# Another order of steps in a chunked attention followed by a multiplicative FFN: S and P of pairs 0 to 3, 6 and 7, turns of x, and some loads

## The chip, the core and the metric

The kernel runs on one core of a Trainium2 chip. The metric is the device time of one execution in microseconds (us). The core's engines run side by side, each through its own list of instructions in order: PE (matrix products, which it writes to PSUM), DVE and ACT (elementwise work), POOL and SP (here they mostly issue DMAs). They wait for each other by semaphores.

## The reference, cut to what matters

```
q, k, v: (8, 8, 576, 64)              # batch, heads, sequence, head size
in chunks of 64 tokens (9 per sequence), per head:
    attn = exp(scores) / (sum + 1e-09),  scores = q @ k.T / 8  (less the row's maximum)
    out  = attn @ v
x = out of all heads side by side      # (4608, 512)
a, b = x @ w1, x @ w2                  # w1, w2: (512, 1024)
result = ((a * b) @ w3) @ w_out        # w3: (1024, 1024), w_out: (1024, 512)
```

## The kernel before, in words

The 4608 tokens are cut into 18 **pairs** of 256 tokens (four chunks). The kernel is one list of steps, `ORDER` (lines 9 to 40), that line 447 goes through; each step issues its instructions at once, and on every engine they run in the order of the list. Nothing else schedules the work: a step that stands earlier in the list stands earlier on each engine that it uses. A letter names the kind of step, the first number is the pair p (or a group of two pairs g = p // 2), the second a part.

| step | engine | what it does (line) |
|---|---|---|
| R0, R1, K0, K1 | SP, ACT | load q and k of pair 0 without a cast, and cast them (135, 141) |
| q, k, v | POOL | loads of a pair, cast to bf16 on the way, in one to three DMAs each (149, 165) |
| i0 to i3, o, h0, h1 | POOL | a quarter of w1 and of w2, w_out, a half of w3 (428, 180, 433) |
| x | POOL | a tiny copy that makes POOL wait until the pair's xn is there (161) |
| T p.0, T p.1 | DVE | turn q and k in blocks of 32 x 32 (195) |
| G g | SP | eight moves that bring the turned blocks together, for pairs 8 and up (205) |
| S p | PE | scores; 64 products of 32 rows (pairs 0 to 7) or 32 of 64 rows (214) |
| E p | ACT | exp (231) |
| P p | PE | exp times v, and the row's sum; 64 or 32 products, in two halves (238) |
| N p.u | DVE | a reciprocal and a product, giving half a pair of x (258) |
| X p.u | DVE | turn half a pair of x (293) |
| H g | SP | eight moves of turned x, for pairs 8 and up (310) |
| A, B p.f | PE | a block of x @ w1, of x @ w2: 8 products of 256 columns for pairs 0 to 3, 4 of 512 for two pairs at a time from pair 4 (326) |
| C p.f | ACT | copy A's result out of PSUM (349) |
| M p.f | DVE | a * b into `ab` (353) |
| V, W, Z | DVE, PE, ACT | turn w3, compute w3 @ w_out once, store it as `w3o` (405 to 420) |
| O p, Y p, Q p | PE, ACT, SP | 16 products of `ab` and `w3o`, the copy out of PSUM, the store (377 to 402) |
| D | PE | filler: products of zeros into a PSUM tile that the next step overwrites (318); D0.1.0.4.512 are 4 of 512 columns |

Five things set who waits for whom:

- **PSUM.** All PSUM tiles come from one pool of four slots (lines 88 and 101). A step that opens a tile waits until the last reader of a slot has run. S is freed by E, each half of P by its N, A and B (one tile) by M, O by Y, W by Z.
- **C and B share a tile.** C reads the half that A wrote. Where C stands ahead of B in the list, PE waits for the copy before B.
- **Buffers in SBUF.** Copies of A have three buffers (line 350), outputs `o_sb` two (395), so Y of one pair waits until the store two before it has landed. q and k have five, v six.
- **POOL's loads.** Each load waits until the load eight before it has landed.
- **SP's queue.** G, H and Q go out in order; a store behind moves leaves after them.

The whole of O16 and O17 stands at the end; O17 goes out in three parts, so that the last store is small. `second_path` (line 453) runs only where a sum was out of range, which it is not here.

Of the kernel before, what the change touches and what calls it, by code (L numbers as in the profile page):

```python
# [7 lines left out]

ORDER = """
R0 R1 v0 q1 k1 i0 v1 i1 i2 q2 k2 v2 i3 q3 k3 v3 q4 k4 v4 o h0 h1 D0.0.0.16.64 K0 T0.0 K1 T0.1 q5 k5  # L10
v5 S0 T1.0 E0 P0 D0.1.0.4.512 T1.1 q6 k6 v6 N0.0 S1 D1.0.0.5.512 X0.0 N0.1 X0.1 A0.0 E1 B0.0 C0.0 P1
M0.0 A0.1 N1.0 X1.0 B0.1 C0.1 N1.1 A0.2 X1.1 B0.2 C0.2 M0.1 A1.0 T2.0 B1.0 C1.0 M0.2 A1.1 T2.1 q7 k7
v7 B1.1 C1.1 M1.0 S2 M1.1 A0.3 E2 T3.0 B0.3 C0.3 P2 M0.3 A1.2 N2.0 X2.0 B1.2 C1.2 N2.1 A1.3 X2.1
B1.3 C1.3 M1.2 A2.0 T3.1 q8 k8 v8 B2.0 C2.0 M1.3 S3 T4.0 A2.1 E3 M2.0 B2.1 T4.1 q9 k9 C2.1 P3 v9
M2.1 A2.2 N3.0 B2.2 C2.2 X3.0 A2.3 N3.1 B2.3 X3.1 C2.3 M2.2 S4 M2.3 A3.0 E4 B3.0 C3.0 A3.1 M3.0 B3.1
C3.1 V0 A3.2 M3.1 B3.2 C3.2 V1 A3.3 M3.2 B3.3 C3.3 V2 W0 M3.3 V3 W1 Z0 V4 V5 W2 Z1 V6 V7 T5.0 Z2 W3
T5.1 q10 k10 T6.0 T6.1 P4 v10 q11 k11 Z3 S5 N4.0 O0 E5 X4.0 N4.1 X4.1 T7.0 O1 T7.1 Y0 Q0 T8.0 P5 v11
q12 k12 Y1 S6 T8.1 O2 Q1 E6 N5.0 X5.0 N5.1 X5.1 O3 T9.0 T9.1 Y2 G4.0 P6 v12 q13 k13 A4.0 N6.0 B4.0
G4.1 Y3 X6.0 N6.1 C4.0 A4.1 X6.1 B4.1 C4.1 M4.0 Q2 S7 Q3 M4.1 A4.2 E7 T10.0 B4.2 C4.2 T10.1 P7 v13
q14 k14 A4.3 M4.2 B4.3 N7.0 C4.3 A4.4 X7.0 M4.3 B4.4 C4.4 N7.1 A4.5 M4.4 B4.5 C4.5 X7.1 S8 M4.5 S9  # L20
E8 A4.6 T11.0 B4.6 E9 T11.1 P8 v14 q15 k15 C4.6 A4.7 M4.6 G5.0 B4.7 C4.7 N8.0 A6.0 M4.7 B6.0 N8.1
C6.0 G5.1 A6.1 X8.0 B6.1 M6.0 C6.1 X8.1 P9 v15 A6.2 M6.1 N9.0 B6.2 C6.2 N9.1 A6.3 M6.2 B6.3 C6.3
X9.0 A6.4 M6.3 B6.4 C6.4 X9.1 A6.5 T12.0 H4.0 B6.5 C6.5 M6.4 A6.6 M6.5 B6.6 T12.1 H4.1 C6.6 S10 S11
M6.6 E10 A6.7 T13.0 B6.7 E11 P10 T13.1 C6.7 O4 M6.7 G6.0 N10.0 N10.1 X10.0 G6.1 P11 Y4 X10.1 O5
N11.0 N11.1 x11 q16 k16 v16 Q4 X11.0 X11.1 T14.0 A8.0 H5.0 Y5 B8.0 T14.1 C8.0 A8.1 M8.0 B8.1 H5.1
C8.1 T15.0 A8.2 B8.2 M8.1 C8.2 T15.1 Q5 A8.3 B8.3 C8.3 M8.2 G7.0 S12 M8.3 S13 E12 A8.4 T16.0 B8.4
E13 G7.1 P12 T16.1 C8.4 A8.5 B8.5 M8.4 C8.5 N12.0 A8.6 M8.5 B8.6 C8.6 N12.1 x12 q17 k17 v17 A8.7
M8.6 B8.7 C8.7 X12.0 P13 M8.7 A10.0 X12.1 B10.0 C10.0 N13.0 A10.1 M10.0 B10.1 N13.1 C10.1 A10.2
X13.0 B10.2 M10.1 C10.2 X13.1 S14 S15 M10.2 E14 A10.3 H6.0 T17.0 B10.3 E15 P14 T17.1 C10.3 A10.4
H6.1 M10.3 B10.4 C10.4 N14.0 A10.5 M10.4 B10.5 G8.0 C10.5 N14.1 A10.6 M10.5 B10.6 C10.6 X14.0 P15  # L30
G8.1 X14.1 A10.7 M10.6 B10.7 N15.0 C10.7 O6 N15.1 M10.7 X15.0 X15.1 H7.0 S16 Y6 S17 O7 E16 E17 H7.1
P16 Y7 O8 Q6 N16.0 Q7 N16.1 X16.0 X16.1 P17 Y8 A12.0 N17.0 Q8 B12.0 N17.1 C12.0 A12.1 X17.0 B12.1
M12.0 C12.1 X17.1 A12.2 M12.1 H8.0 B12.2 C12.2 A12.3 M12.2 B12.3 C12.3 H8.1 A12.4 M12.3 B12.4 C12.4
A12.5 M12.4 B12.5 C12.5 A12.6 M12.5 B12.6 C12.6 A12.7 M12.6 B12.7 C12.7 O9 M12.7 O10 Y9 Q9 A14.0 Y10
B14.0 C14.0 Q10 A14.1 M14.0 B14.1 C14.1 A14.2 M14.1 B14.2 C14.2 A14.3 M14.2 B14.3 C14.3 A14.4 M14.3
B14.4 C14.4 A14.5 M14.4 B14.5 C14.5 A14.6 M14.5 B14.6 C14.6 A14.7 M14.6 B14.7 C14.7 O11 M14.7 O12
Y11 Q11 A16.0 Y12 B16.0 C16.0 Q12 A16.1 M16.0 B16.1 C16.1 A16.2 M16.1 B16.2 C16.2 A16.3 M16.2 B16.3
C16.3 A16.4 M16.3 B16.4 C16.4 A16.5 M16.4 B16.5 C16.5 A16.6 M16.5 B16.6 C16.6 A16.7 M16.6 B16.7
C16.7 O13 M16.7 O14 Y13 Q13 O15 Y14 Q14 O16 Y15 Q15 Y16 Q16 O17
"""  # L40


# [525 lines left out]
```

## Time and profile before

| | |
|---|---|
| median of 3 runs | 244.46 us (244.37 to 244.63) |
| profiled execution | 244.48 us, of which the span of the profile is 242.9 |
| PE busy | 226.7 us, 2753 products |
| DVE, ACT, POOL busy | 154.3, 85.2, 83.7 us |
| granted PE clock | 1.0 over the span |
| 71 copies C, 586 ns each | 41.6 us of ACT |
| 71 products M, 674 ns each | 47.8 us of DVE |
| 36 turns T, 1291 ns each | 45.1 us of DVE |
| chain that ended last | PE 72%, DMA 16%, DVE 4%, SP's queue 3% |

How to read the views: a timeline line gives start, length, engine, source line, operation, tiles written and read, and the number of instructions merged; in brackets stands the idle time of the engine just before it and what ended it. "Issue" is idle time for which the profile shows no releaser. All products have one source line, that of a helper, so the tile names tell the steps apart: `z_ps` are the fillers and the tiles that they opened, `s_ps` S, `pv` P, `ab_ps` A and B, `o_ps` O, `qkT` T, `xt` and `xm` X. Source lines are those of this kernel; the changed list is one line shorter.

### The profile page before, as it was taken

Reading aid. Unit: us, or ns where it says so; the run is one execution under the profiler, and the core shown is the slowest. Engines: PE = TensorE matmul, PEld = TensorE weight load, DVE = VectorE, ACT = ScalarE, POOL = GpSimd, SP = SyncE. Lnnn points to the kernel's source line nnn. Section 1 sums busy time; section 2 is a strip of 40 time slices with the busy share of each in tenths; the row PEclk is TensorE's granted clock in tenths of the full one; section 3 lists DMA queues with packets and bytes.
Section 4 is the critical chain, followed back from the end, with each engine's and each line's share of the span. In section 5 each row is a group of like instructions: output and inputs, shape, how many; then the busy total and the mean of one; then the engine's idle time right before and its main releaser. Section 6 shows DMA issues by size and latency. Waiting matters only on the chain.

```text
span 242.9 us, 6385 instructions
## 1 busy us (share of the span) xinstructions
PE 226.7 (93%) x2753; PEld 120.2 (49%) x2753; DVE 154.3 (64%) x235; ACT 85.2 (35%) x116; POOL 83.7 (34%) x114
## 2 busy tenths in 40 slices
...
GB/s 173 179 185 181 185 169 200 196 193 171 167 173 218 222 228 259 179 224 196 205 236 223 221 139 91 163 88 209 142 0 89 87 0 0 173 3 1 86 173 173
DMA packets 93597, 37.65 MB, mean 155 GB/s; under 512 B 75008, under 2 KB 86528, under 8 KB 93568
## 3 DMA queue, kind: packets, MB, share of 16 engines
...
q8 instruction: 21, 0.34, 0.6%
...
## 4 chain that ended last, share of the span: by engine, by line
PE 72%; DMA 16%; DVE 4%; SPq 3%; POOL 2%; issue 1%; ACT 0%; DVEq 0%; POOLq 0%
PE ab_ps L95 39%; PE o_ps L95 23%; PE w_ps L95 6%; DMA w<-in_moe_w_dram 4%; DMA qkm<-qkT 3%; SPq L193 3%; DMA qk<-in_q_dram 3%; DMA qk<-in_k_dram 3%; DMA xt<-xm 3%; PE pv L95 2%; PE s_ps L95 2%; DVE qkT L201 2%; POOL vbuf L98 1%; POOL w L98 1%; DVE xt L297 1%
## 5 line engine op out<-in xcount | busy, mean ns | idle before, releaser
L95 PE MATMUL ab_ps<-xt,w 128*128 128x512 bf16 (+1 forms) x688 | 127.4, 342 | 0.7 <-DVE xt L297 0.6
L95 PEld LDWEIGHTS <-w 128*128 128x128 bf16 x704 | 67.1, 98 | 56.1 <-issue 1.8
L366 DVE TENSOR_TENSOR ab<-a_sb,ab_ps 128x512 bf16<-128x512 f32 x71 | 47.8, 674 | 43.4 <-ACT a_sb L351 43.1
L351 ACT COPY a_sb<-ab_ps 128x512 f32<-128x512 f32 x71 | 41.6, 586 | 81.3 <-PE ab_ps L95 81.0
L95 PE MATMUL o_ps<-w3o,ab 128*128 128x512 bf16 (+1 forms) x296 | 63.9, 373 | 0.0
L201 DVE STREAM_TRANSPOSE qkT<-qk 128x1024 bf16<-128x1024 bf16 x36 | 45.1, 1291 | 7.2 <-ACT qk L144 5.5
L95 PEld LDWEIGHTS <-ab 128*128 128x128 bf16 x296 | 28.5, 98 | 32.2
L98 POOL DMA_DIRECT2D vbuf<-in_v_dram x40 | 33.9, 855 | 20.4 <-DMA qk<-in_q_dram 5.2
L396 ACT COPY o_sb<-o_ps 128x1024 f32<-128x1024 f32 x17 | 17.2, 1012 | 45.3 <-PE o_ps L95 41.3
L264 DVE TENSOR_TENSOR xn<-pv,rcs 128x512 bf16<-128x512 f32 x36 | 24.9, 692 | 1.4
...
L234 ACT ACTIVATE e<-s_ps 128x1024 bf16<-128x1024 f32 x16 | 15.9, 1026 | 1.7 <-PE s_ps L95 1.3
L95 PE MATMUL w_ps<-wo,w3T 128*128 128x512 bf16 x64 | 14.0, 379 | 0.0
L305 DVE STREAM_TRANSPOSE xm<-xn 128x512 bf16<-128x512 bf16 x20 | 13.5, 696 | 0.2
L261 DVE RECIPROCAL rcs<-pv 128x8 f32<-128x8 f32 x36 | 6.9, 193 | 10.4 <-PE pv L95 10.4
L98 POOL DMA_DIRECT2D w<-in_moe_w_dram x16 | 11.1, 695 | 5.3 <-DMA wo<-in_moe_w_out_dram 2.9
...
L95 PE MATMUL pv<-vbuf,e 64*32 64x65 bf16 (+1 forms) x832 | 10.2, 197 | 1.8 <-ACT e L234 1.1
L297 DVE STREAM_TRANSPOSE xt<-xn 128x512 bf16<-128x512 bf16 x16 | 11.4, 711 | 0.5
L389 DVE COPY o_sb<-o_ps 128x256 f32<-128x256 f32 x1 | 0.4, 425 | 16.0 <-PE o_ps L95 16.0
L95 PEld LDWEIGHTS <-qkT 32*64 32x64 bf16 x512 | 5.5, 117 | 10.1 <-DVE qkT L201 7.9
...
## 6 DMA issues: line engine op xcount, KB each, us to landing
...
```

The source lines that it names most:

```text
L95: return inorder(nc.tensor.matmul(*a, **kw))
L98: return inorder(nc.gpsimd.dma_start(dst, src))
L193: inorder(nc.sync.dma_start(dst, src))
L201: inorder(nc.vector.transpose(qkT_t[g][:, :, p % 2, s, heads(h)].rearrange("p e h (y t) -> p h t e y", t=2), qk_t[p][:, s, heads(h)].rearr ...
L234: inorder(nc.scalar.activation(e_t[p][:, :, heads(hh)], s_t[p][:].rearrange("p u (h q) -> p u h q", q=CH)[:, :, heads(hh)], Exp, scale=sca ...
L261: inorder(nc.vector.reciprocal(rc, pv[:, :, :, D:W]))
L264: inorder(nc.vector.tensor_mul(xn_t[p][:, u], pv[:, :, :, 0:D], rc.to_broadcast([P, 2, 4, D])))
L297: inorder(nc.vector.transpose(new_xt(g)[:].rearrange("p (o t) -> p o t", o=KO)[:, :, t0:t0 + UT] .rearrange("p o (m y) -> p m o y", y=BL), ...
L305: inorder(nc.vector.transpose(xm_t[g][:, u, :, m].rearrange("p o (c y) -> p c o y", y=BL), xn_t[p][:].rearrange("p u r m d -> p (u r) m d" ...
L351: inorder(nc.scalar.copy(a_t[p, j][:], ps_t[p, j][:, 0, :]))
L366: inorder(nc.vector.tensor_mul(o, view(a_t.pop((p, j))[:]), view(ps_t.pop((p, j))[:, 1, :])))
L396: inorder(nc.scalar.copy(o_sb[:], ps_t.pop(p)[:]))
```

## The change

Only the list changes. The 606 steps stay the same but for the three fillers: D0.0.0.16.64 becomes D0.0.0.24.64 and stands ahead of h0, D0.1.0.4.512 becomes D0.1.0.6.512, D1.0.0.5.512 becomes D1.0.0.1.512 and stands ahead of P0. In the order:

- S and P of pairs 0 to 3, 6 and 7 change places with blocks A and B: S1 stands behind A0.0, P1 behind A0.1, S2 behind A0.3, P2 behind A1.2, S7 behind A4.2, P7 behind A4.3; likewise P8 behind A4.6, P12 behind A8.5, P14 behind A10.4, P17 behind A12.0.
- Turns X, and N, stand ahead of some products M: both N of pair 2 ahead of both X, X1.1 ahead of M0.0, X15.0 and X15.1 ahead of M10.7, X16 and X17.1 ahead of M12.0.
- Blocks change places (A1.1 ahead of A1.0, A8.3 ahead of A8.1, O10 inside A12's blocks, O14 inside A16's), and six copies C stand ahead of their B (1.0, 1.2, 1.3, 3.3, 6.0, 8.3).
- Turns T change places (T6.1 ahead of T5.0, T13.1 ahead of T13.0 and T12.1, T17.0 ahead of M10.2, X5.0 behind T9), and V6 ahead of V4. E4 stands behind Z2, E13 ahead of E12, Y14 ahead of Y13.
- Loads change places from k6 on (k6 ahead of v5 and q6, v11 ahead of k11, k12 ahead of q12, v12 behind q13, q16, k16 and v16 ahead of x11, k17 behind v17); Q3 stands ahead of Q2 on SP.

The diff, cut to the stretches where these stand:

```
--- before
+++ after
-R0 R1 v0 q1 k1 i0 v1 i1 i2 q2 k2 v2 i3 q3 k3 v3 q4 k4 v4 o h0 h1 D0.0.0.16.64 K0 T0.0 K1 T0.1 q5 k5
-v5 S0 T1.0 E0 P0 D0.1.0.4.512 T1.1 q6 k6 v6 N0.0 S1 D1.0.0.5.512 X0.0 N0.1 X0.1 A0.0 E1 B0.0 C0.0 P1
-M0.0 A0.1 N1.0 X1.0 B0.1 C0.1 N1.1 A0.2 X1.1 B0.2 C0.2 M0.1 A1.0 T2.0 B1.0 C1.0 M0.2 A1.1 T2.1 q7 k7
-v7 B1.1 C1.1 M1.0 S2 M1.1 A0.3 E2 T3.0 B0.3 C0.3 P2 M0.3 A1.2 N2.0 X2.0 B1.2 C1.2 N2.1 A1.3 X2.1
-B1.3 C1.3 M1.2 A2.0 T3.1 q8 k8 v8 B2.0 C2.0 M1.3 S3 T4.0 A2.1 E3 M2.0 B2.1 T4.1 q9 k9 C2.1 P3 v9
+R0 R1 v0 q1 k1 i0 v1 i1 i2 q2 k2 v2 i3 q3 k3 v3 q4 k4 v4 o D0.0.0.24.64 h0 h1 K0 T0.0 K1 T0.1 q5 S0 E0
+T1.0 T1.1 k5 D1.0.0.1.512 k6 v5 P0 q6 N0.0 D0.1.0.6.512 X0.0 N0.1 X0.1 A0.0 S1 E1 B0.0 C0.0 A0.1 v6 P1
+N1.0 X1.0 N1.1 X1.1 M0.0 B0.1 T2.0 A0.2 C0.1 B0.2 T2.1 C0.2 M0.2 q7 A1.1 A1.0 C1.0 B1.1 v7 B1.0 C1.1
+M1.0 M1.1 M0.1 A0.3 S2 T3.0 B0.3 E2 k7 C0.3 M0.3 A1.2 P2 C1.2 A1.3 N2.0 v8 N2.1 X2.0 X2.1 B1.2 C1.3 T3.1
+B1.3 A2.0 q8 k8 B2.0 S3 C2.0 M1.2 A2.1 M1.3 T4.0 E3 M2.0 B2.1 P3 T4.1 q9 v9 A2.2 N3.0 C2.1 B2.2 A2.3
...
-T5.1 q10 k10 T6.0 T6.1 P4 v10 q11 k11 Z3 S5 N4.0 O0 E5 X4.0 N4.1 X4.1 T7.0 O1 T7.1 Y0 Q0 T8.0 P5 v11
-q12 k12 Y1 S6 T8.1 O2 Q1 E6 N5.0 X5.0 N5.1 X5.1 O3 T9.0 T9.1 Y2 G4.0 P6 v12 q13 k13 A4.0 N6.0 B4.0
-G4.1 Y3 X6.0 N6.1 C4.0 A4.1 X6.1 B4.1 C4.1 M4.0 Q2 S7 Q3 M4.1 A4.2 E7 T10.0 B4.2 C4.2 T10.1 P7 v13
-q14 k14 A4.3 M4.2 B4.3 N7.0 C4.3 A4.4 X7.0 M4.3 B4.4 C4.4 N7.1 A4.5 M4.4 B4.5 C4.5 X7.1 S8 M4.5 S9
-E8 A4.6 T11.0 B4.6 E9 T11.1 P8 v14 q15 k15 C4.6 A4.7 M4.6 G5.0 B4.7 C4.7 N8.0 A6.0 M4.7 B6.0 N8.1
+N4.0 S5 Z3 T6.0 E5 T7.1 q11 X4.0 O0 N4.1 X4.1 T8.0 Y0 Q0 T7.0 O1 P5 Y1 v11 S6 O2 N5.0 k11 T8.1 k12 N5.1
+E6 X5.1 Q1 O3 q12 T9.1 T9.0 G4.0 k13 P6 X5.0 A4.0 Y2 q13 B4.0 G4.1 N6.0 Y3 N6.1 X6.0 C4.0 A4.1 B4.1 X6.1
+v12 A4.2 C4.1 M4.0 Q3 M4.1 Q2 S7 E7 B4.2 C4.2 A4.3 P7 T10.0 T10.1 q14 B4.3 v13 M4.2 N7.0 A4.5 X7.0 C4.3
+A4.4 M4.3 B4.4 C4.4 B4.5 C4.5 N7.1 k14 X7.1 M4.4 S8 S9 M4.5 E8 q15 A4.6 P8 T11.0 B4.6 T11.1 k15 E9 C4.6
+M4.6 A4.7 N8.0 B4.7 C4.7 A6.0 A6.1 v14 M4.7 N8.1 G5.0 X8.0 C6.0 G5.1 B6.0 B6.1 M6.0 C6.1 M6.1 P9 v15
...
-X13.0 B10.2 M10.1 C10.2 X13.1 S14 S15 M10.2 E14 A10.3 H6.0 T17.0 B10.3 E15 P14 T17.1 C10.3 A10.4
...
-G8.1 X14.1 A10.7 M10.6 B10.7 N15.0 C10.7 O6 N15.1 M10.7 X15.0 X15.1 H7.0 S16 Y6 S17 O7 E16 E17 H7.1
-P16 Y7 O8 Q6 N16.0 Q7 N16.1 X16.0 X16.1 P17 Y8 A12.0 N17.0 Q8 B12.0 N17.1 C12.0 A12.1 X17.0 B12.1
+B10.1 A10.2 k17 C10.1 X13.0 M10.1 B10.2 C10.2 S14 S15 A10.3 E14 X13.1 H6.0 T17.0 M10.2 B10.3 E15 A10.4
+T17.1 H6.1 C10.3 P14 G8.0 B10.4 M10.3 N14.0 C10.4 A10.5 M10.4 B10.5 N14.1 C10.5 A10.6 G8.1 B10.6 M10.5
+X14.1 C10.6 X14.0 P15 A10.7 B10.7 O6 M10.6 C10.7 N15.0 N15.1 X15.0 X15.1 H7.0 S16 S17 E16 O7 P16 M10.7
+Y6 E17 Y7 H7.1 O8 A12.0 Q6 P17 A12.1 N16.0 Q7 Y8 N16.1 N17.0 B12.0 N17.1 X16.0 A12.2 X16.1 Q8 C12.0
...
```

More of the change, by code (lines that the diff above doesn't have):

```diff
@@ L15 @@
-M2.1 A2.2 N3.0 B2.2 C2.2 X3.0 A2.3 N3.1 B2.3 X3.1 C2.3 M2.2 S4 M2.3 A3.0 E4 B3.0 C3.0 A3.1 M3.0 B3.1
-C3.1 V0 A3.2 M3.1 B3.2 C3.2 V1 A3.3 M3.2 B3.3 C3.3 V2 W0 M3.3 V3 W1 Z0 V4 V5 W2 Z1 V6 V7 T5.0 Z2 W3
-T5.1 q10 k10 T6.0 T6.1 P4 v10 q11 k11 Z3 S5 N4.0 O0 E5 X4.0 N4.1 X4.1 T7.0 O1 T7.1 Y0 Q0 T8.0 P5 v11
-q12 k12 Y1 S6 T8.1 O2 Q1 E6 N5.0 X5.0 N5.1 X5.1 O3 T9.0 T9.1 Y2 G4.0 P6 v12 q13 k13 A4.0 N6.0 B4.0
-G4.1 Y3 X6.0 N6.1 C4.0 A4.1 X6.1 B4.1 C4.1 M4.0 Q2 S7 Q3 M4.1 A4.2 E7 T10.0 B4.2 C4.2 T10.1 P7 v13
@@ L20 @@
-q14 k14 A4.3 M4.2 B4.3 N7.0 C4.3 A4.4 X7.0 M4.3 B4.4 C4.4 N7.1 A4.5 M4.4 B4.5 C4.5 X7.1 S8 M4.5 S9
-E8 A4.6 T11.0 B4.6 E9 T11.1 P8 v14 q15 k15 C4.6 A4.7 M4.6 G5.0 B4.7 C4.7 N8.0 A6.0 M4.7 B6.0 N8.1
[L22 to L25, printed above, removed]
@@ L26 @@
-C8.1 T15.0 A8.2 B8.2 M8.1 C8.2 T15.1 Q5 A8.3 B8.3 C8.3 M8.2 G7.0 S12 M8.3 S13 E12 A8.4 T16.0 B8.4
-E13 G7.1 P12 T16.1 C8.4 A8.5 B8.5 M8.4 C8.5 N12.0 A8.6 M8.5 B8.6 C8.6 N12.1 x12 q17 k17 v17 A8.7
-M8.6 B8.7 C8.7 X12.0 P13 M8.7 A10.0 X12.1 B10.0 C10.0 N13.0 A10.1 M10.0 B10.1 N13.1 C10.1 A10.2
-X13.0 B10.2 M10.1 C10.2 X13.1 S14 S15 M10.2 E14 A10.3 H6.0 T17.0 B10.3 E15 P14 T17.1 C10.3 A10.4
-H6.1 M10.3 B10.4 C10.4 N14.0 A10.5 M10.4 B10.5 G8.0 C10.5 N14.1 A10.6 M10.5 B10.6 C10.6 X14.0 P15
-G8.1 X14.1 A10.7 M10.6 B10.7 N15.0 C10.7 O6 N15.1 M10.7 X15.0 X15.1 H7.0 S16 Y6 S17 O7 E16 E17 H7.1
@@ L32 @@
-P16 Y7 O8 Q6 N16.0 Q7 N16.1 X16.0 X16.1 P17 Y8 A12.0 N17.0 Q8 B12.0 N17.1 C12.0 A12.1 X17.0 B12.1
[L33 to L36, printed above, removed]
@@ L37 @@
-Y11 Q11 A16.0 Y12 B16.0 C16.0 Q12 A16.1 M16.0 B16.1 C16.1 A16.2 M16.1 B16.2 C16.2 A16.3 M16.2 B16.3
-C16.3 A16.4 M16.3 B16.4 C16.4 A16.5 M16.4 B16.5 C16.5 A16.6 M16.5 B16.6 C16.6 A16.7 M16.6 B16.7
-C16.7 O13 M16.7 O14 Y13 Q13 O15 Y14 Q14 O16 Y15 Q15 Y16 Q16 O17
+R0 R1 v0 q1 k1 i0 v1 i1 i2 q2 k2 v2 i3 q3 k3 v3 q4 k4 v4 o D0.0.0.24.64 h0 h1 K0 T0.0 K1 T0.1 q5 S0 E0
+T1.0 T1.1 k5 D1.0.0.1.512 k6 v5 P0 q6 N0.0 D0.1.0.6.512 X0.0 N0.1 X0.1 A0.0 S1 E1 B0.0 C0.0 A0.1 v6 P1
+N1.0 X1.0 N1.1 X1.1 M0.0 B0.1 T2.0 A0.2 C0.1 B0.2 T2.1 C0.2 M0.2 q7 A1.1 A1.0 C1.0 B1.1 v7 B1.0 C1.1
@@ new lines @@
+M1.0 M1.1 M0.1 A0.3 S2 T3.0 B0.3 E2 k7 C0.3 M0.3 A1.2 P2 C1.2 A1.3 N2.0 v8 N2.1 X2.0 X2.1 B1.2 C1.3 T3.1
+B1.3 A2.0 q8 k8 B2.0 S3 C2.0 M1.2 A2.1 M1.3 T4.0 E3 M2.0 B2.1 P3 T4.1 q9 v9 A2.2 N3.0 C2.1 B2.2 A2.3
+B2.3 N3.1 M2.1 X3.0 k9 X3.1 C2.3 M2.3 C2.2 S4 A3.0 B3.0 C3.0 M2.2 A3.3 M3.0 A3.1 B3.1 C3.3 C3.1 V0 A3.2
+M3.1 V1 B3.2 V3 V2 C3.2 B3.3 M3.3 W0 V6 W1 Z0 V4 V5 M3.2 Z1 W2 T6.1 Z2 V7 T5.0 W3 T5.1 E4 q10 P4 v10 k10
+N4.0 S5 Z3 T6.0 E5 T7.1 q11 X4.0 O0 N4.1 X4.1 T8.0 Y0 Q0 T7.0 O1 P5 Y1 v11 S6 O2 N5.0 k11 T8.1 k12 N5.1
@@ new lines @@
+E6 X5.1 Q1 O3 q12 T9.1 T9.0 G4.0 k13 P6 X5.0 A4.0 Y2 q13 B4.0 G4.1 N6.0 Y3 N6.1 X6.0 C4.0 A4.1 B4.1 X6.1
+v12 A4.2 C4.1 M4.0 Q3 M4.1 Q2 S7 E7 B4.2 C4.2 A4.3 P7 T10.0 T10.1 q14 B4.3 v13 M4.2 N7.0 A4.5 X7.0 C4.3
+A4.4 M4.3 B4.4 C4.4 B4.5 C4.5 N7.1 k14 X7.1 M4.4 S8 S9 M4.5 E8 q15 A4.6 P8 T11.0 B4.6 T11.1 k15 E9 C4.6
+M4.6 A4.7 N8.0 B4.7 C4.7 A6.0 A6.1 v14 M4.7 N8.1 G5.0 X8.0 C6.0 G5.1 B6.0 B6.1 M6.0 C6.1 M6.1 P9 v15
+A6.2 B6.2 N9.0 C6.2 N9.1 X8.1 M6.2 A6.3 B6.3 A6.4 X9.0 C6.3 X9.1 B6.4 T12.0 A6.5 H4.0 C6.4 B6.5 C6.5
@@ new lines @@
+A6.6 M6.4 B6.6 M6.3 M6.5 T13.1 C6.6 q16 T12.1 M6.6 S10 E10 H4.1 S11 A6.7 B6.7 P10 E11 k16 C6.7 O4 N10.0
+M6.7 T13.0 G6.0 N10.1 X10.0 T14.0 G6.1 Y4 P11 O5 N11.0 X10.1 N11.1 v16 x11 Q4 A8.0 B8.0 A8.3 X11.0 Y5
+C8.0 H5.0 X11.1 H5.1 T14.1 T15.1 A8.1 Q5 M8.0 B8.1 C8.3 C8.1 A8.2 B8.2 T15.0 B8.3 C8.2 M8.1 M8.2 S12
+G7.0 S13 M8.3 E13 A8.4 T16.0 E12 B8.4 G7.1 A8.5 C8.4 P12 B8.5 M8.4 A8.6 N12.0 B8.6 T16.1 C8.5 A8.7 C8.6
+M8.5 N12.1 M8.6 q17 X12.1 x12 B8.7 v17 C8.7 P13 N13.0 X12.0 A10.0 B10.0 C10.0 M8.7 A10.1 N13.1 M10.0
```

7 lines of the change are left out of this document (added).

## The prediction, made before the changed kernel ran

> **What bounds the kernel now.** I read the busy row and the queues of the page first, then the timeline of PE from end to end for its holes, and then, at each hole, the timelines of the engine that ended it.
>
> ```profile
> PE 226.7 (93%) x2753; PEld 120.2 (49%) x2753; DVE 154.3 (64%) x235; ACT 85.2 (35%) x116; POOL 83.7 (34%) x114
> ...
> q8 instruction: 21, 0.34, 0.6%
> ```
>
> PE is busy for 226.7 of 242.9 us. Of the other 16.2, 9.9 are ahead of 12.02 (1.4 to the first filler, 7.4 for the first turns, 1.1 for E0) and 3.2 behind the last product. Neither end moves: loads, turns and copies up to X0.1 stand in the same order, and so do O16 and O17 with their stores. So the change can only touch the holes between 12 and 240 us, and make new ones. These are the holes (start, length, what ran, and the idle time before it):
>
> ```profile
> 14.52 1.02 PE L95 MATMUL z_ps<-qkT 32*64 32x64 bf16 x64
> 15.48 1.25 PE L95 MATMUL z_ps<-zero 128*128 128x512 bf16 x5
> 16.57 0.82 PE L95 MATMUL z_ps<-xt,w 128*128 128x256 bf16 x6
> 18.51 1.25 PE L95 MATMUL z_ps<-xt,w 128*128 128x256 bf16 x10 [1.12 <-issue]
> ...
> 24.31 3.67 PE L95 MATMUL ab_ps<-xt,w 128*128 128x256 bf16 x32 [0.33 <-DVE xt L297]
> ...
> 31.53 0.30 PE L95 MATMUL pv<-vbuf,e 64*32 64x65 bf16 x27 [0.67 <-issue]
> 31.76 3.67 PE L95 MATMUL ab_ps<-xt,w 128*128 128x256 bf16 x32
> 35.71 1.92 PE L95 MATMUL ab_ps<-xt,w 128*128 128x256 bf16 x16 [0.29 <-DVE xt L297]
> ```
> ```profile
> 86.63 0.60 PE L95 MATMUL s_ps<-qkT 32*64 32x64 bf16 x51
> 87.72 0.31 PE L95 MATMUL s_ps<-qkT 32*64 32x64 bf16 x13 [0.49 <-issue]
> ```
>
> "Issue" means that no semaphore held PE. The three such holes (1.12, 0.67 and 0.49 us) come after 447, 957 and 2744 of PE's instructions (each product is two, a weight load and a matmul): 510 and 1787 apart, within 5 of 2 and 7 times 256. [...] I read each hole as a refill that came late. A small product takes 10 ns (64 in 0.64 us), so S or P eats 128 instructions in 0.6 us; a block lasts longest where FFN products stand between. [...]
>
> **The change, part by part.** Times below are places in the profiled execution of before. Prices: an 8-product block of 256 columns 0.87 us (64 in 7.09, less 0.1 for the switch from a small block), a block of four with 512 columns 0.86 (64 in 13.81), a 32-row S or P 0.64, a 64-row one 0.38. The FFN products are the same in number, and the runs of small products go from 28 to 29, so PE's work is unchanged but for fillers.
>
> 1. *Pairs 0 to 3.* Fillers: 8 more narrow ones lie in the 7.4 us hole; the wide ones go from 9 to 7. Behind P0 (ends 12.7) six take 0.43 to 0.45 each (four took 1.81) and end at 15.3; X0.1 ends at 15.79 as before, A0.0 starts at 15.84 (before 16.57) and S1 follows at 16.7. Nothing is won: the 447th instruction is now the 57th product of S1, reached at 17.3, and the refill, asked for around P0's start, frees PE at 18.50 as before. The granted speed had doubled by 15.5 (0.45 against 0.22 us for a wide filler); a doubling that came later would hide behind the same refill up to 18.50, so I take 0, and 0.3 as the worst. From 18.50: rest of S1 0.1, B0.0 and A0.1 1.85, so P1 starts at 20.4. Its first half frees N1.0 at 20.85 (before 21.02, behind M0.0), and the 3.23 us of two N and two X end at 24.1: A1.1 starts 0.15 sooner than A1.0 did. Four blocks reach 27.6; A0.3 waits for its weights, which landed at 27.80; then A0.3, S2, B0.3, A1.2 bring P2 to 31.2. The second block border has moved 24 products into P2, 5.5 us after the border before it (4.9 with the hole), so the 0.67 hole goes. What is late next is M0.3: it stands behind T3.0, which waits for q3.
>
> ```profile
> 30.64 1.31 DVE L201 STREAM_TRANSPOSE qkT<-qk 128x1024 bf16<-128x1024 bf16 x1 [1.32 <-DMA qk<-in_q_dram]
> 31.86 0.65 DVE L366 TENSOR_TENSOR ab<-a_sb,ab_ps 128x512 bf16<-128x512 f32 x1
> ```
>
> Loads up to q5 keep their order, so M0.3 still ends at 32.5, and A1.3, now directly behind P2 (31.8), waits 0.7 for its PSUM slot. The hole has changed its name. Both N then stand ahead of both X, which saves two waits of 0.1; X2.1 ends at about 35.45 against 35.65, and A2.0 is 0.2 ahead. Up to A3.0 nothing binds that did not. **Term 1: -0.2** (bounds -0.4 and +0.3).
>
> 2. *Pairs 6 and 7.* A4.2 now stands ahead of S7, so between the border near P6 and the next one PE has 0.86 us more to do: the border in S7 comes some 6.2 us after the last (5.3 with the hole). The hole goes, and with it the slow restart (the 13 products behind it took 0.31): S7 took 1.33 instead of 0.64. **-0.7.** The next block is shorter, 7.25 us instead of 8.16. Its packet ran at 92.8 to 93.9 in before, 5.1 us after the hole; in the three holes the first instruction came 1.3 to 1.6 us after the packet's end, which would be 7.5. A hole of 0 to 0.4 in S8: I take **+0.15**.
>
> 3. *Loads.* v11 (three DMAs) now stands ahead of k11. In their places v11 landed at 96.2 to 97.7, so k11 lands near 97.7 instead of 94.5. T11.1 began at 98.2 and, with terms 1 and 2, would begin near 97.5: a wait of 0 to 1. Behind it stand M4.6 (A6.0 waits for it, 0.23 us to spare), N8.0 and, by SP, the moves G5, the last of which landed at 112.89, when S10 wanted it. I take **+0.25**. q16, k16 and v16 leave ahead of the tick of x11, some 5 us sooner, beside G6: G6 landed by 124.8, S12 needs it at 130.5, which covers it. Q3 ahead of Q2 changes no store that anyone waits for.
>
> 4. *Order of M, C, E, T.* Six C now stand ahead of their B (same PSUM tile), so PE waits for ACT's copy: 0.1 + 0.59 + 0.05 us against a block of 0.86 between them, so nothing, with 0.1 to spare. E13 ahead of E12 ends E12 at 133.1; P12, behind A8.5 now, wants it at 133.7. M6.6 stands behind T13.1 and T12.1 and ends at 115.6; P10's second half wants it at 115.9. M10.2 stands behind T17.0 (145.18 + 1.22 + 0.67 = 147.0), and A10.4, now ahead of P14, wants it at 146.93: **+0.1**. Bounds 0 and 0.6, since several have only 0.1 to 0.3 to spare.
>
> 5. *P17.* It now stands between A12.0 and A12.1, with B12.0 behind. A12.1 needs the PSUM slot that Y8 frees, and Y8 waited for a store:
>
> ```profile
> 157.06 6.07 SPq L193 DMA_DIRECT2D xt<-xm  x8
> 163.23 5.78 SPq L193 DMA_DIRECT2D out_dram<-o_sb  x3
> ```
> ```profile
> 167.60 1.01 ACT L396 COPY o_sb<-o_ps 128x1024 f32<-128x1024 f32 x1 [4.04 <-DMA out_dram<-o_sb]
> ```
>
> Y8 ended at 168.61; A12.1 stood at 168.58 and lost 0.1. In the new order PE is there at 166.39 + 0.86 + 0.38 + 0.1 = 167.7: a wait of 0.95 if Y8 stays, 0.85 more than before. But Q6 is late because it stands on SP behind H7, which starts when X15.0 ends, and X15.0 now stands ahead of M10.7 (0.68): Q6 leaves at 162.55, lands at 166.9 and Y8 ends at 167.9 or sooner. **+0.1** (0 to 0.85).
>
> **Sum:** -0.2 - 0.7 + 0.15 + 0.25 + 0.1 + 0.1 = -0.3. The profiled execution took 244.48 us (span 242.9 and 1.6 around it), the median of the runs is 244.46. So 244.2.
>
> **Rivals.** *Faster:* the refill holes go and the covers of terms 3 to 5 hold (k11 in time, 0.1 at most in each): -0.2 - 0.7 + 0.1 = -0.8, 243.7. For it: PE's other holes are under 0.2 us. Against: S10 already waited for G5 before. *Slower:* k11 holds T11.1. In the trace loads land in the order of issue, and between 83 and 98 us G4, Q2 and Q3 share the DMA engines with them (SP's moves took 7 us to land, loads 13). If k11 lands at 98.9 in place of 97.7, T11.1 runs to 100.2 and M4.6 to 100.8, where A6.0, due at 99.5, waits 1.3 in place of the 0.25 I took: -0.3 + 1.05 = +0.75, 245.2. It ends above the band from a landing at 98.7 on. For it: k11 is the larger load (192 and 64 KB against 64, 64 and 128 of v11). Against: the bytes are the same, 256 KB. The full wait at A12.1 (SP paused 1.2 us between H7.0 and H7.1 with nothing named, which may eat the 0.68) gives -0.3 + 0.75 = +0.45, 244.9: alone it stays inside the band. *The holes are no refills:* 87.7 keeps its hole, term 2 is 0 and the sum +0.25, 244.7. *One wait for another:* where every hole only changes its name, as P2's does at A1.3, the time stays at 244.5.
>
> **How the numbers follow.** About 0.2% (0.5 us) is what a measurement of this kernel can tell from no change. My forecast, 244.2, has 0.26 and the three rivals that end inside the band 0.16 together: 0.42. Faster than 243.97 gets 0.34. Slower than 244.95 gets 0.24: 0.14 for k11 alone, 0.10 for its smaller delays beside the wait at A12.1. The range runs from 243.4 (term 1 at -0.4, term 2 at -0.7, little given back) to 245.3 (terms 3 to 5 near their upper bounds).
>
> **What would show it.** Right: no "issue" hole in P2 and S7; a wait of 0.7 on A1.3 behind M0.3 at 32.5; A2.0 near 35.5; A12.1 stalled less than 0.4. Wrong: holes of over 0.5 us in S8, S10 or A12.1, T11.1 waiting for k11 past 98.5, or a first refill that frees PE at another time than 18.5.

## The result, and the profile after

The changed kernel takes **245.72 us** (median of 20 runs, 244.15 to 246.43) where the kernel before takes 244.61 beside it (20 runs): a ratio of 1.0040, 95% interval 1.0027 to 1.0054. It is slower by 0.3 to 0.5%, where the prediction had it 0.3 us faster, at 244.2 (243.4 to 245.3). Its profiled execution took 245.46 us, 243.9 of them the span.

The page of the changed kernel: busy time by engine, the instruction queue q8, and, in the list of DMA issues, the moves G with the median of issue to landing at the end of the line (4.0 us in before).

```profile
PE 228.9 (94%) x2759; PEld 120.9 (50%) x2759; DVE 152.3 (62%) x235; ACT 84.5 (35%) x116; POOL 83.9 (34%) x114
...
q8 instruction: 22, 0.36, 0.6%
...
qkm<-qkT SPq DMA_DIRECT2D x40, 128.0 KB, 6.5
```

PE's products are the same but for fillers. That PE is busy 2.2 us longer is partly A0.0, which ran at half speed (1.85 us for eight products, 1.03 at full speed; it cost nothing, see the end), and partly groups stretched by waits inside them (S8, S12). The moves G need 2.5 us more to land: that is the first hint.

Where is it lost? I lined the two traces up by work. For every step I added up what PE had done ahead of it (one price for each kind of step) and read when before had done as much. The difference is the **lag**: negative, and the changed kernel is ahead. (Where small and large groups stand in another order, as just ahead of A4.7, 0.2 of it may be the order.)

| at | A2.0 | O2 | A4.0 | A4.7 | S12 | A10.0 | O8 | A12.2 | end |
|---|---|---|---|---|---|---|---|---|---|
| lag, us | -0.30 | -0.13 | 0.15 | -0.42 | -0.09 | 0.63 | 0.63 | 0.97 | 0.98 |

At S12, 130 us into the span, the changed kernel is still ahead. It loses 0.7 in S12 and 0.35 at A12.1, and next to nothing else up to the end. The lines (start, length, engine, operation, tiles, count, idle time before and what ended it): first the timeline of PE near its start.

```profile
15.86 1.85 PE L94 MATMUL z_ps<-xt,w 128*128 128x256 bf16 x8 [0.40 <-DVE xt L296]
17.65 0.71 PE L94 MATMUL z_ps<-qkT 32*64 32x64 bf16 x64
...
27.80 1.05 PE L94 MATMUL ab_ps<-xt,w 128*128 128x256 bf16 x8 [0.20 <-DMA w<-in_moe_w_dram]
28.77 0.70 PE L94 MATMUL s_ps<-qkT 32*64 32x64 bf16 x64
29.41 1.92 PE L94 MATMUL ab_ps<-xt,w 128*128 128x256 bf16 x16
31.26 0.70 PE L94 MATMUL pv<-vbuf,e 64*32 64x65 bf16 x64
32.52 4.71 PE L94 MATMUL ab_ps<-xt,w 128*128 128x256 bf16 x39 [0.56 <-DVE ab L365]
```

S1 (17.65) and P2 (31.26) run through; the holes without a releaser are gone. A1.3 waits 0.56 behind M0.3 instead. The same timeline around pairs 6 to 8:

```profile
83.22 4.49 PE L94 MATMUL ab_ps<-xt,w 128*128 128x512 bf16 x20 [0.21 <-DVE xt L296]
87.64 0.70 PE L94 MATMUL s_ps<-qkT 32*64 32x64 bf16 x64
...
95.21 0.98 PE L94 MATMUL s_ps<-qkm 64*64 64x64 bf16 x64
```

S7 (87.64) has no hole. But A4.0 now waits for X5.0, and the 64 products of S8 and S9 take 0.98 (0.71 in before). DVE shows what held X5.0:

```profile
80.11 2.49 DVE L200 STREAM_TRANSPOSE qkT<-qk 128x1024 bf16<-128x1024 bf16 x2 [1.88 <-DMA qk<-in_k_dram]
82.49 0.67 DVE L296 STREAM_TRANSPOSE xt<-xn 128x512 bf16<-128x512 bf16 x1
```

T9.1 waited 1.9 us for the load k9, which now stands behind v9: it landed at 80.08 (75.56 in before, where T9.0 began at 77.83 and T9.1 at 79.00). X5.0, which stood ahead of T9 in before, is behind both turns. Then S12, on PE, in before and in the changed kernel:

```profile
130.50 0.71 PE L95 MATMUL s_ps<-qkm 64*64 64x64 bf16 x64
```
```profile
130.41 0.21 PE L94 MATMUL s_ps<-qkm 64*64 64x64 bf16 x1
130.87 0.93 PE L94 MATMUL s_ps<-qkm 64*64 64x64 bf16 x63 [0.25 <-DMA qkm<-qkT]
```

One product, then a wait for a move G6, then 63 products in 0.93 where 64 usually take 0.71: the second, third and fourth start at 130.87, 131.00 and 131.12, and the rest at the usual pace. The last move had landed at 130.73; what spaces these three the trace doesn't name. On SP the eight moves G6 left here, in before and in the changed kernel:

```profile
116.89 5.79 SPq L193 DMA_DIRECT2D qkm<-qkT  x8
```
```profile
118.83 5.50 SPq L192 DMA_DIRECT2D qkm<-qkT  x8
```

In before the last of them landed at 124.78; now it lands at 130.73. On DVE the turns of pair 13 ran one behind the other in before. Now T13.0, for which SP waited, stands behind N10.0 and M6.7:

```profile
114.36 2.46 DVE L201 STREAM_TRANSPOSE qkT<-qk 128x1024 bf16<-128x1024 bf16 x2
```
```profile
116.25 0.69 DVE L263 TENSOR_TENSOR xn<-pv,rcs 128x512 bf16<-128x512 f32 x1
116.86 0.68 DVE L365 TENSOR_TENSOR ab<-a_sb,ab_ps 128x512 bf16<-128x512 f32 x1
117.45 1.31 DVE L200 STREAM_TRANSPOSE qkT<-qk 128x1024 bf16<-128x1024 bf16 x1
```

Last, A12.1 on PE:

```profile
166.93 1.03 PE L94 MATMUL ab_ps<-xt,w 128*128 128x512 bf16 x4
167.88 0.45 PE L94 MATMUL pv<-vbuf,e 64*64 64x65 bf16 x32
168.78 3.40 PE L94 MATMUL ab_ps<-xt,w 128*128 128x512 bf16 x15 [0.45 <-ACT o_sb L395]
```

A12.0, P17, and 0.45 of waiting for Y8, which itself waited for the store Q6 (landed 167.61; 167.50 in before).

### The profile page after: what moved, and what is told of

Read it like the earlier page. It is cut to its first block, busy times and chain, and to the rows that moved or that the text cites. A ratio compares the mean times of both kernels' runs of the same rounds, so it can differ in the third digit from the quotient of the medians.

```text
span 243.9 us, 6399 instructions
## 1 busy us (share of the span) xinstructions
PE 228.9 (94%) x2759; PEld 120.9 (50%) x2759; DVE 152.3 (62%) x235; ACT 84.5 (35%) x116; POOL 83.9 (34%) x114
## 4 chain that ended last, share of the span: by engine, by line
PE 48%; DMA 28%; POOL 7%; DVE 5%; SPq 5%; issue 5%; ACT 1%; POOLq 0%; DVEq 0%; ACTq 0%
PE ab_ps L94 33%; PE o_ps L94 13%; DMA w<-in_moe_w_dram 8%; DMA qk<-in_k_dram 7%; SPq L192 5%; DMA qk<-in_q_dram 4%; DMA qkm<-qkT 4%; POOL vbuf L97 3%; DMA vbuf<-in_v_dram 3%; DVE qkT L200 2%; DMA out_dram<-o_sb 2%; POOL qk L97 2%; PE s_ps L94 1%; DVE xm L304 1%; DVE ab L365 1%
## 5 line engine op out<-in xcount | busy, mean ns | idle before, releaser
L365 DVE TENSOR_TENSOR ab<-a_sb,ab_ps 128x512 bf16<-128x512 f32 x71 | 46.8, 673 | 47.0 <-ACT a_sb L350 46.6
L296 DVE STREAM_TRANSPOSE xt<-xn 128x512 bf16<-128x512 bf16 x16 | 10.9, 696 | 0.3
L406 DVE STREAM_TRANSPOSE w3T<-w 128x1024 bf16<-128x1024 bf16 x8 | 9.4, 1212 | 1.5 <-DMA w<-in_moe_w_dram 1.5
```

Source lines behind the costliest of these rows:

```text
L296: inorder(nc.vector.transpose(new_xt(g)[:].rearrange("p (o t) -> p o t", o=KO)[:, :, t0:t0 + UT] .rearrange("p o (m y) -> p m o y", y=BL), ...
L365: inorder(nc.vector.tensor_mul(o, view(a_t.pop((p, j))[:]), view(ps_t.pop((p, j))[:, 1, :])))
L406: inorder(nc.vector.transpose(w3T_t[f][:].rearrange("p k (f y) -> p f k y", y=BL), w3[:, NB * f:NB * (f + 1), :].rearrange("p f (k x) -> p ...
```

## The experiments

All times are medians beside the kernel before, which took 244.54 to 244.60 in these comparisons. In the cut diffs a moved step is shown where it stands now, and not always where it stood. My theory after the result: three delays that the prediction had missed or taken too low, (1) k9 behind v9, (2) G6 late, (3) B12.0 behind A12.1, each a gate at a fixed time, set by a transfer, that takes back whatever PE has won ahead of it. The rivals stand with each run.

**A12.1: whose place makes the wait?** First B12.0 back ahead of A12.1:

```
-O8 A12.0 Q6 P17 A12.1 N16.0 Q7 Y8 N16.1 N17.0 B12.0 N17.1
+O8 A12.0 Q6 P17 B12.0 A12.1 N16.0 Q7 Y8 N16.1 N17.0 N17.1
```

> The changed kernel with B12.0 put back ahead of A12.1 (behind P17), nothing else. Theory (PSUM slot): A12.1 needs the slot that Y8 frees at 168.73; with B12.0 in between PE reaches A12.1 at about 169.1, so the 0.45 us hole at A12.1 goes and PE ends 0.35 us sooner: 0.35 us under the changed kernel in its profile, about 245.4 against 245.7. Rival (the store of pair 6 only moves the wait): A12.1 or the block behind it still stands for over 0.3, and PE ends where it did.

245.05 us, ratio 1.0026 (1.0006 to 1.0046). The wait at A12.1 is gone; from O8 to A12.2 the lag grows by 0.10 instead of 0.34. (This profile's end is no sooner than the changed kernel's, since A4.0 and S8 lost 1.5 in it, 1.0 more than there.) Then P17 alone:

```
-O7 P16 M10.7 Y6 E17 Y7 H7.1 O8 A12.0 Q6 P17 A12.1
+O7 P16 M10.7 Y6 E17 Y7 H7.1 O8 P17 A12.0 Q6 A12.1
```

> The changed kernel with P17 put back ahead of A12.0 (behind O8), nothing else; B12.0 stays behind A12.1. Theory (PSUM slot): the three tiles of P17, A12.0 and A12.1 take the same three slots in a row as before, so A12.1 still waits until Y8 ends (about 168.7): a hole of 0.4 to 0.5 stays and the time is that of the changed kernel within 0.1 us. Rival (my prediction's wording, that P17's place makes the wait): the hole goes, 0.35 us less.

245.51 us, ratio 1.0046 (1.0033 to 1.0059; 6 runs). The time is the changed kernel's, as the theory had it, but its profile has no hole at A12.1, which the theory had wrong: in that execution, the fastest of the six, Q6 landed 3.7 us after it left (4.3 to 5.1 in the others where it stands behind H7.1), and Y8 was done in time. So this run leaves the question open; e9_p17 below settles it.

**S12: the late turn or the early loads?** T13.0 back ahead of N10.0 and M6.7, then, by itself, the loads back behind x11:

```
-M6.6 S10 E10 H4.1 S11 A6.7 B6.7 P10 E11 k16 C6.7 O4 N10.0 M6.7 T13.0 G6.0
+M6.6 T13.0 S10 E10 H4.1 S11 A6.7 B6.7 P10 E11 k16 C6.7 O4 N10.0 M6.7 G6.0
```

> The changed kernel with T13.0 moved from behind M6.7 to directly behind M6.6 on DVE; the loads stay. Theory (late moves): SP issues G6 when the last turn of pairs 12 and 13 ends; T13.0 would end near 116.7 instead of 118.74, G6 leave near 116.8 instead of 118.83 and land near 128 or sooner instead of 130.73, so S12 no longer waits (its 0.25 hole and slow 0.93 go) and PE is 0.6 to 0.7 us ahead at A8.4. At A12.1 some of it is given back, as Y8 waits for a store that hangs on SP: 0.3 to 0.7 less at the end. Rival (loads): q16, k16 and v16 beside G6 make it slow, whenever it leaves; then G6 lands near 130 still and the time stays within 0.2 of the changed kernel.

```
-A6.6 M6.4 B6.6 M6.3 M6.5 T13.1 C6.6 q16 T12.1 M6.6
+A6.6 M6.4 B6.6 M6.3 M6.5 T13.1 C6.6 T12.1 M6.6
...
-P10 E11 k16 C6.7
+P10 E11 C6.7
...
-N11.0 X10.1 N11.1 v16 x11 Q4
+N11.0 X10.1 N11.1 x11 q16 k16 v16 Q4
```

> The changed kernel with the loads q16, k16 and v16 put back behind x11 (and its wait on POOL), T13.0 left where it is. Rival (loads beside G6): G6, issued at 118.8 to 123.7, lands in 3 to 4 us each, the last near 127.5 instead of 130.73, S12 does not wait, 0.6 to 0.7 less at A8.4 and 0.3 to 0.7 less at the end. Theory (late moves alone): G6 still lands near 130.5, S12 stands, and the time stays within 0.2 of the changed kernel.

T13.0: 245.27 us, ratio 1.0029 (1.0020 to 1.0038); G6 left at 116.79 and landed at 129.15. The loads: 245.04 us, 1.0019 (1.0000 to 1.0037); G6 left at 118.70, as late as in the changed kernel, and landed at 126.41. S12 on PE, first with T13.0 moved, then with the loads moved:

```profile
130.67 0.71 PE L94 MATMUL s_ps<-qkm 64*64 64x64 bf16 x64
```
```profile
130.40 0.71 PE L94 MATMUL s_ps<-qkm 64*64 64x64 bf16 x64
```

Both are whole. In the five profiles that keep both the late turn and the early loads, G6 landed at 130.31 to 131.08, and S12 lost 0.37 to 0.79 in four of them and nothing in one where PE came late. So both rivals are half right: it takes the late turn and the early loads together to make S12 wait, and either put back is enough. The loads weigh more: taken back by themselves they give G6 4.3 us, the turn 1.6. And the end? O8 is at a lag of 0.16 and -0.11 instead of 0.63, but A12.1 waits 0.88 and 0.61 instead of 0.45: Q6 landed at 167.58 and 167.03. With the turn put back, the second wait took all that the first had let through (0.94 at the end); with the loads, 0.15 of 0.74 (0.39 at the end).

**k9 alone.**

```
-P3 T4.1 q9 v9 A2.2 N3.0 C2.1 B2.2 A2.3 B2.3 N3.1 M2.1 X3.0 k9 X3.1
+P3 T4.1 q9 k9 v9 A2.2 N3.0 C2.1 B2.2 A2.3 B2.3 N3.1 M2.1 X3.0 X3.1
```

> The changed kernel with the load k9 moved back ahead of v9 (directly behind q9), nothing else. Theory (k9, not k11): k9 lands near 77 instead of 80.1, T8.1, T9.1 and T9.0 end before 80.5 instead of 82.6, X5.0 no longer holds A4.0 and G4 leaves near 80.5 and lands near 92.5 instead of 95.1, so S8 does not stand: 0.3 less at A4.0 and 0.5 to 0.6 less at A4.7. S10 gives 0.3 to 0.5 of it back, since the moves G5 still land near 112; at the end 0 to 0.2 less than the changed kernel, whose other losses (S12, A12.1) stay. Rival (my term 3: k11 behind v11): S8 and A4.0 stand as they do, no difference over 0.1 at A4.7.

245.53 us, ratio 1.0029 (1.0011 to 1.0048). k9 landed at 75.75, A4.0 did not wait, and A4.7 has a lag of -0.86 (-0.42 in the changed kernel). Here T11.1, no longer late for other reasons, waited 0.74 for k11 (landed 97.97), and A6.0 gave 0.2 back, waiting for M4.6. What is left, -0.48 at S12, goes there:

```profile
130.02 0.21 PE L94 MATMUL s_ps<-qkm 64*64 64x64 bf16 x1
130.59 0.93 PE L94 MATMUL s_ps<-qkm 64*64 64x64 bf16 x63 [0.36 <-DMA qkm<-qkT]
```

Where the changed kernel came to S12 at 130.40 and lost 0.69, this one came 0.39 sooner and lost 0.79. That is a gate, but not one at a fixed time: G6 left sooner here too and landed at 130.45 instead of 130.73. So the lead over before is gone behind S12 (a lag of 0.29 at A10.0), while most of the lead over the changed kernel (0.63 there) passed. I had expected S10 to be the gate; it was S12. The median, 245.53, is not told apart from the changed kernel's: what k9 costs stands in the traces, and no time shows it by itself.

**Term 2 alone, in the kernel before,** and the head of the change alone:

```
-C4.1 M4.0 Q2 S7 Q3 M4.1 A4.2 E7
+C4.1 M4.0 Q2 A4.2 S7 Q3 M4.1 E7
```

> The kernel before with A4.2 moved ahead of S7, nothing else. Theory: the hole without a releaser in S7 (0.49) and its slow restart go, 0.6 to 0.7 less at B4.3 (term 2 of the prediction); at S8 and S10 it is given back, as S10 needs G5, which landed at 112.89 when S10 wanted it: the end within 0.15 of before. Rival 1 (holes are no refills): the hole stays in S7. Rival 2 (gain stays): 0.5 or more less at the end, 244.0.

244.48 us, ratio 0.9993 (0.9982 to 1.0003). PE:

```profile
88.16 0.71 PE L95 MATMUL s_ps<-qkT 32*64 32x64 bf16 x64
...
113.17 1.23 PE L95 MATMUL s_ps<-qkm 64*64 64x64 bf16 x64
```

S7 runs through, and the lag falls from 0.66 to 0.22 there (this execution had lost 0.7 ahead of A2.0; with one block between S7 and P7, P7 waits 0.17 for E7). S10 gives 0.23 back: 1.23 instead of 1.00, with G5's last landing at 113.33 (112.89 in before). So the hole goes with one moved block, and half of the gain is gone at the next gate.

For the head, `ORDER` of the changed kernel up to S4 (with k9 ahead of v9), and then all other steps as in before:

```
-C2.1 P3 v9 M2.1 A2.2 N3.0 B2.2 C2.2 X3.0 A2.3 N3.1 B2.3 X3.1 C2.3 M2.2 S4 M2.3 A3.0
+P3 T4.1 q9 k9 v9 A2.2 N3.0 C2.1 B2.2 A2.3 B2.3 N3.1 M2.1 X3.0 X3.1 C2.3 M2.3 C2.2 S4 M2.2 A3.0
```

> The kernel before with the changed order up to S4 only (pairs 0 to 3 and their fillers, k9 left ahead of v9), the rest as before. Theory (S10 is a gate set by transfers): 0.2 to 0.3 less from A2.0 to S9, and nothing of it behind S10, since G5 lands when it did (112.9): the end within 0.1 of before. Rival (what is won early stays won): 0.2 to 0.3 less at the end, 244.3.

244.48 us, ratio 1.0007 (0.9990 to 1.0024): no difference that shows. Its one profile has no lead at A2.0 (0.00; -0.26 to -0.38 in ten of the eleven kernels that have the changed head in full, -0.06 in one), so it can't tell a kept gain from a lost one. On the head it is inconclusive. The same profile, the fastest of the twelve runs, says something on S7, around which the order is that of before:

```profile
86.59 0.54 PE L95 MATMUL s_ps<-qkT 32*64 32x64 bf16 x44
87.29 0.35 PE L95 MATMUL s_ps<-qkT 32*64 32x64 bf16 x20 [0.16 <-issue]
```

The hole comes 7 products sooner in S7, and 6 more fillers have run ahead of it: counted in PE's instructions it is at the same place within two (2742 and 2744). That speaks for a border in the instruction stream, though no view names one. The size of the hole varies: 0.16 here, 0.49 in the profile of before. And the 0.35 that S7 lost less here were kept to the end, as G5 had landed at 111.44, ahead of S10 at 112.57: a gate takes back only where its transfer is late.

**All four edits undone together** (k9, T13.0, the three loads, B12.0).

```
-P3 T4.1 q9 v9 A2.2
+P3 T4.1 q9 k9 v9 A2.2
...
-M6.6 S10 E10 H4.1
+M6.6 T13.0 S10 E10 H4.1
...
-N11.1 v16 x11 Q4
+N11.1 x11 q16 k16 v16 Q4
...
-P17 A12.1 N16.0
+P17 B12.0 A12.1 N16.0
```

> The changed kernel with four edits undone: k9 ahead of v9; T13.0 directly behind M6.6; q16, k16, v16 behind x11; B12.0 ahead of A12.1. Theory (these are all that it lost): 0.3 to 0.5 less than before up to S10, 0.1 to 0.4 less behind it, no stand at S12, at most 0.2 at A12.1; 244.2 to 244.6, so 1.0 to 1.4 less than the changed kernel. Rival (the many other swaps cost too): holes at other places, over 0.5 more than before at the end.

**244.13 us, ratio 0.9978 (0.9966 to 0.9989)**: 1.6 us under the changed kernel, and faster than before by 0.1 to 0.3%. The lag is -0.89 at A4.7, -0.82 at S12 and -0.80 at O8: next to nothing is given back any more. G6 landed at 125.64, and A12.1 did not wait. The many other swaps of the change cost nothing that shows.

**A12.1 again: P17 in place of B12.0,** the other three edits undone as above:

```
-O8 A12.0 Q6 P17 B12.0 A12.1 N16.0 Q7 Y8 N16.1 N17.0 N17.1
+O8 P17 A12.0 Q6 A12.1 N16.0 Q7 Y8 N16.1 N17.0 B12.0 N17.1
```

> The kernel with four edits undone (e8_undo4), but with P17 put back ahead of A12.0 in place of B12.0 ahead of A12.1. Theory (PSUM slot, three tiles in a row): A12.1 takes the third slot as in the changed kernel and waits until Y8 ends, near 167.2 to 168.7, where PE is ready at 166.7: a hole of 0.4 to 1.2 at A12.1, and 0.4 to 0.9 more at the end than e8_undo4 (244.13 there). Rival (P17's place makes the wait): no hole, the time of e8_undo4.

244.51 us, ratio 0.9995 (0.9975 to 1.0014), 0.4 more; the intervals overlap, so the trace has to decide. PE:

```profile
165.89 0.45 PE L94 MATMUL pv<-vbuf,e 64*64 64x65 bf16 x32
166.27 1.04 PE L94 MATMUL ab_ps<-xt,w 128*128 128x512 bf16 x4
167.95 4.26 PE L94 MATMUL ab_ps<-xt,w 128*128 128x512 bf16 x19 [0.64 <-ACT o_sb L395]
```

P17 stands where it stood in before, and A12.1 still waits for Y8. P17, A12.0 and A12.1 open three tiles in a row, and the third slot is Y8's in either order; what covers the wait is B12.0, which writes into A12.0's tile and needs no new one.

**The gate itself: the store ahead of the moves.** The changed kernel with Q6 moved on SP only:

```
-P16 M10.7 Y6 E17 Y7 H7.1 O8 A12.0 Q6 P17 A12.1
+P16 M10.7 Y6 Q6 E17 Y7 H7.1 O8 A12.0 P17 A12.1
```

> The changed kernel with the store Q6 moved directly behind Y6 in the list, so ahead of the moves H7.1 on SP, nothing else. Theory (Y8 waits for Q6's landing, and Q6 for SP): Q6 leaves near 160 instead of 162.87 and lands before 165.5 instead of 167.61, Y8 starts when O8 ends (near 167.0) instead of 167.71 and the hole at A12.1 (0.45) goes: 0.3 less at the end, with nothing changed ahead of it. Rival (the store's landing is set by the traffic beside it, or Y8 then waits for Q7): Y8 still starts near 167.7 and the hole stays.

245.01 us, ratio 1.0019 (1.0006 to 1.0032). SP, and then ACT:

```profile
156.87 3.76 SPq L192 DMA_DIRECT2D xt<-xm  x4
160.99 0.38 SPq L192 DMA_DIRECT2D out_dram<-o_sb  x1
161.47 2.53 SPq L192 DMA_DIRECT2D xt<-xm  x4
```
```profile
166.82 1.01 ACT L395 COPY o_sb<-o_ps 128x1024 f32<-128x1024 f32 x1 [2.97 <-PE o_ps L94]
```

The store left between the halves of H7 and landed at 163.88 instead of 167.61. Y8 is now released by O8's products, not by the store, and PE goes through A12.1 without a wait (lag 0.28 at O8, 0.13 at the end). The price is that H7.1 landed at 166.69 instead of 164.17; its x is not needed before A14.0, at 187.6. In this execution PE came to S12 at 130.78, when G6 had landed (130.37), and lost nothing there: late already, it had nothing to give back.

**Two more edits undone,** on top of the four:

```
-Y1 v11 S6 O2 N5.0 k11 T8.1
+Y1 k11 v11 S6 O2 N5.0 T8.1
...
-W0 V6 W1 Z0 V4 V5 M3.2 Z1 W2
+W0 W1 Z0 V4 V5 M3.2 V6 Z1 W2
```

> e8_undo4 with two more edits undone: the load k11 ahead of v11, and V6 behind M3.2 on DVE instead of ahead of W1. Theory: V5 ends 1.2 sooner, so the hole of 0.2 at W2 goes; k11 lands near 95 instead of 97.6, T11.1 starts before 97 and the loss of 0.27 between A4.7 and B6.1 goes (term 3 of the prediction as it stood); 0.3 to 0.5 less than e8_undo4 at S12 if nothing gives it back, 243.7 to 243.9. Rival (gates behind them, G5 at S10 or the store at Y8): the same time as e8_undo4.

243.99 us, ratio 0.9969 (0.9953 to 0.9985); not told apart from 244.13. k11 landed at 94.36 instead of 97.64, but T11.1 started only 0.23 sooner and the lag at A4.7 and S12 is what it was (-0.86, -0.86): behind its load stand the turns and products ahead of it on DVE. The pause of 0.2 in W1 is there in some executions and not in others, with V6 in either place; I can't name its cause. With Q6 behind Y6 as well:

```
-Y6 E17 Y7 H7.1 O8 A12.0 Q6 P17
+Y6 Q6 E17 Y7 H7.1 O8 A12.0 P17
```

> e11_k11v6 with the store Q6 directly behind Y6 as well. Theory: Y8 no longer waits for the store, so what PE won ahead of A12 reaches the end whole: 0.1 to 0.4 less than e11_k11v6, 243.4 to 243.8, the fastest of all. Rival: with B12.0 ahead of A12.1 the store is covered already, the same time as e11_k11v6.

243.79 us, ratio 0.9982 (0.9962 to 1.0001). The store landed at 162.68 and A12.1 did not wait (0.33 in e11_k11v6's profile), but the times of the two don't differ by more than their spread. The three versions with all four edits undone beat the changed kernel. The first two also beat before clear of noise, the interval of the third reaches 1.0001; which of the three is best, the runs don't say. (In each of the last four traces 23 records of products are missing; their places in the lags are taken from the weight loads.)

The lags side by side:

| kernel | A2.0 | A4.0 | A4.7 | S12 | A10.0 | O8 | end | time minus that of before |
|---|---|---|---|---|---|---|---|---|
| changed | -0.30 | 0.15 | -0.42 | -0.09 | 0.63 | 0.63 | 0.98 | 1.1 |
| B12.0 back | -0.34 | 0.41 | 0.34 | 0.35 | 0.93 | 0.93 | 1.03 | 0.5 |
| T13.0 back | -0.06 | 0.43 | -0.28 | 0.17 | 0.15 | 0.16 | 0.94 | 0.7 |
| loads back | -0.29 | 0.01 | -0.11 | -0.10 | -0.12 | -0.11 | 0.39 | 0.5 |
| k9 back | -0.31 | -0.34 | -0.86 | -0.48 | 0.29 | 0.32 | 0.59 | 1.0 |
| Q6 early | -0.37 | 0.27 | 0.03 | 0.29 | 0.28 | 0.28 | 0.13 | 0.4 |
| four undone | -0.31 | -0.07 | -0.89 | -0.82 | -0.80 | -0.80 | -0.96 | -0.4 |
| P17 for B12.0 | -0.26 | -0.01 | -0.55 | -0.50 | -0.49 | -0.49 | 0.15 | -0.1 |

Read each row from left to right: where the number rises, PE lost time. A profile is one execution, and the store and the moves land some tenths sooner or later in each, so a row's end need not be the median's difference.

## Why the prediction was wrong, point by point

The forecast of -0.3 had the gains right and missed what the moved transfers took back. Between -0.3 and the 0.98 of the two profiles lie above all S12 (0.69, forecast at nothing), A4.0 (0.28, in no term) and A12.1 (0.25 over its term).

1. *Pairs 0 to 3, -0.2:* -0.3. The holes went and A1.3 waited 0.56 behind M0.3 (0.7 forecast). One step failed: I had the first refill free PE at 18.50 as before; its packet came at 14.5 (16.2 in before) and S1 ran at 17.65 without a hole. Why it came sooner stays open: no run shows when a refill is asked for. It changed little, as the turns of pair 1 and then the weights at 27.80 set the pace again.
2. *S7, -0.7 and +0.15:* right, against this one profile of before. The hole and slow restart are gone in every kernel with A4.2 ahead of S7, e7_s7 with nothing else changed. From A4.0 to B4.4 the lag falls by 0.64 (0.62 to 0.69 in all eleven kernels with the changed middle part). But e6_head, with before's order there, lost 0.35 less in S7, so the gain differs from one execution to the next. The next border does what was feared: in e4_k9, S8 pauses 0.16 with no releaser, some 250 instructions behind the place of before's hole in S7, though G4 had landed 1.5 us before S8 began. That a hole is a late refill stays my reading. The prediction's 256 is no measured number: if q8 is PE's alone, the two pages give an estimate of 262 instructions to a packet in before (5506 to 21) and of 251 in the changed kernel (5518 to 22). And with 21 packets in before only three such holes show, in A0.0, P2 and S7 (1.12, 0.67 and 0.49 us).
3. *Loads, +0.25 for k11:* the wrong load. In the changed kernel k11 landed at 96.73, 1.0 ahead of T11.1. The mechanism is real: in e4_k9, where DVE is there sooner, k11 held T11.1 and cost the 0.2 at A6.0 that the term foresaw; but putting k11 back (e11_k11v6) changed nothing that shows. The load that hurt first was **k9 behind v9**, which I listed in no term, nor among the moved loads of the change: 0.28 at A4.0, and through G4 (left at 82.62, before 80.29) part of what S8 lost: 0.1 to 0.8 in the six profiles with k9 behind v9, 0 to 0.4 in the five with it ahead (all with the changed middle part).
4. *G6, the step that failed:* "q16, k16 and v16 leave ahead of the tick of x11, some 5 us sooner, beside G6: G6 landed by 124.8, S12 needs it at 130.5, which covers it." That took G6's landing from the trace of before as if it stayed. But the changed list has T13.0 behind N10.0 and M6.7, and G6 is issued when the last turn of its pairs ends: 1.94 later; and the loads that I had just put beside it made it land at 130.73. A cover of 5.7 us was gone, and S12 lost 0.69. I priced the moved turn only by M6.6, which stood behind it, and not by the DMAs that wait for it.
5. *Order of M, C, E, T, +0.1:* 0; A10.4 did not wait.
6. *P17, +0.1 (0 to 0.85):* 0.35, inside its bounds, and by the mechanism that I gave, the slot that Y8 frees. What I hoped for, that X15.0's earlier place lets Q6 leave sooner, came (162.87, before 163.23), but the store took 4.7 us to land instead of 4.3. The term's name was wrong: it is B12.0's place, not P17's, that counts (e9_p17).

Of the signs against it, one came, the first refill at another time. A12.1 stood for 0.45, over the 0.4 that I had called right, and the hole that decided, in S12, was not on the list.
